# States in small groups, x cast by its load, transposes a batch ahead, outputs on another queue: a cross-attention and maxout kernel

## The chip, the cores and the metric

One core of a Trainium2 chip. The metric is the device time in microseconds of one execution, the median of several runs. A profile of one execution gives the times inside it; its span runs from the first to the last instruction.

## What is computed

For every batch b (8) and head h (8), with S = 512 tokens, Ns = 32 states and D = 64:

```
scores  = x @ state.T / 8          # 512 x 32
xread   = softmax(scores) @ state  # 512 x 64
scores2 = state @ x.T / 8          # 32 x 512
sread   = softmax(scores2) @ x     # 32 x 64
a = concat(xread, sread)           # 544 tokens, heads side by side: 512 features
out = max(a @ w1, a @ w2, a @ w3) @ w_out     # 512 -> 768 -> 512
```

All inputs and outputs are float32; x is 8.4 MB, the four weight matrices 6.3 MB together, the output 8.9 MB.

## The kernel before, in words

The kernel works in bf16 and batch by batch. Tokens stand four to a partition row (`J = 4`), heads in pairs: `g` is the position in a pair, `s` the pair. The states stand transposed in block-diagonal pairs (`bd`), so that one 128-row operand serves both scores and the products with the weights.

The steps of a batch, each a helper:

- `load_x(b)` (L75): x from HBM to bf16 by a casting DMA on GpSimd's queue.
- `x_transpose` (L153, on PE, with a copy from PSUM by the engine handed in) or `x_transpose_dma` (L165, a DMA transpose on SP's queue): xT.
- `scores` (L169): 16 matmuls of 64 columns (L181), then exp on ACT (L186) into `e`. `softmax` (L188): sum (L193) and reciprocal (L195) on DVE, multiplication into `a` on the engine handed in (L196; GpSimd from batch 2 on).
- `a_transpose` (PE, L201) or `a_transpose_dma` (SP, L210): aT.
- `g_cols(b, ms)` (L236): G, the states of the batch times columns of the weights. One m (128 of the 768 hidden columns) is 8 small matmuls (L244) and a copy from PSUM by ACT of 768 columns (L248).
- `x_maxout(b, m)` (L266): six matmuls of 512 columns (L258) into three PSUM tiles `pw`; ACT casts the first (L262), DVE takes two maxima (L263, L264) into `ht`.
- `sread(b)` (L215): 32 matmuls, two DVE operations, and a DMA transpose on SP into `ats`. At the end `s_maxout` puts the rows of all batches through the weights.
- `ffn_out(b, j)` (L276): six matmuls (L281), a copy to `osb` by ACT (L288), and for every two j an output DMA (L297) on SP.

The tiles `pw` and all transposes share four PSUM buffers; `pg`, `ps` and the keep-busy matmuls share two pairs of banks. The order of each engine's and each queue's work is the order of the program text (`manual_schedule`). The top part (L303 to L339) writes out batch 0 and the preparation of batch 1. From L343 on, `x_maxout(b, m)` for six m is followed by what stands in `slots[m]`: the preparation of batch n = b + 1, and `ffn_out` of the batch before from `pending`.

The states are prepared twice: `states_first` (L122) for batch 0, `states_rest` (L132) for all others, called after the first maxout of batch 0 (L316). `keep_busy(n)` (L113) issues n matmuls of 512 columns on zeros. Weights come in three chunks of hidden columns, (0,1), (1,3), (3,6), each three casting DMAs on GpSimd.

Of the kernel before, what the change touches and what calls it, by code (L numbers as in the profile page):

```python
# [8 lines left out]
F32 = mybir.dt.float32  # L9
# [6 lines left out]
def kernel(  # L16
# [36 lines left out]
    ctx.enter_context(tc.manual_schedule())  # L53


    st0_f = data.tile([128, 2, D], F32, name="st0f")
    nc.scalar.dma_start(out=st0_f, in_=state[0].rearrange("h n d -> (h n) d").rearrange("(t p) d -> p t d", p=128))
    x0_f = [data.tile([128, HS, J * D], F32, name=f"x0f{g}") for g in range(2)]
    for g in range(2):
        nc.sync.dma_start(  # L60
            out=x0_f[g], in_=x[0].rearrange("(s g) (p j) d -> g p s (j d)", g=2, j=J)[g])
    st_f = data.tile([128, 16, D], F32, name="stf")
    nc.sync.dma_start(
        out=st_f, in_=state.rearrange("b h n d -> (b h n) d").rearrange("(p t) d -> p t d", t=16))

    zero = const.tile([128, 512], BF16, name="zero")
    nc.vector.memset(zero, 0.0)
    ident = const.tile([128, 128], BF16, name="ident")
    make_identity(nc, ident)


    x_sb = [data.tile([128, XW + D], BF16, name=f"x{b}") for b in range(B)]
# [4 lines left out]
            out=x_sb[b][:, 0:XW].rearrange("p (h jd) -> p h jd", h=H),  # L77
            in_=x[b].rearrange("h (p j) d -> p h (j d)", j=J))

    chunks = ((0, 1), (1, 3), (3, 6))  # L80
    w_sb = [wpool.tile([128, HS, 3, (m1 - m0) * 128], BF16, name=f"w{m0}") for m0, m1 in chunks]
    wout_sb = wpool.tile([128, NM, d_model], BF16, name="wout")

# [13 lines left out]
    load_w(1)
    bd0 = data.tile([128, H, 2, Ns], BF16, name="bd0")
    nc.vector.memset(bd0, 0.0)
    bdr = data.tile([128, B - 1, H, 2, Ns], BF16, name="bdr")  # L100
    for b in range(B):
        nc.vector.memset(x_sb[b][:, XW:XW + D], 1.0)
    load_w(2)
    load_x(1)
    nc.gpsimd.dma_start(out=wout_sb, in_=moe_w_out.rearrange("(kk p) f -> p kk f", p=128))
    nc.gpsimd.memset(bdr, 0.0)
    load_x(2)

    warm = const.tile([128, 1], F32, name="warm")
    nc.scalar.activation(out=warm, in_=zero[:, 0:1], func=AF.Exp, scale=1.0)  # L110
# [6 lines left out]


    def bd(b, h):
        return bd0[:, h] if b == 0 else bdr[:, b - 1, h]  # L120

    def states_first():  # L122
        st0 = data.tile([128, 2, 2, D], BF16, name="st0")
        nc.vector.tensor_copy(out=st0, in_=st0_f.unsqueeze(2).to_broadcast((128, 2, 2, D)))
        p = pp.tile([128, 2, 128], BF16, tag="pw", bufs=4, name="pt0")
        for t in range(2):
            nc.tensor.transpose(p[:, t, :], st0[:, t].rearrange("p c d -> p (c d)"), ident)
        for c, copy in enumerate((nc.vector.tensor_copy, nc.scalar.copy)):
            r = slice(64 * c, 64 * c + 64)
            copy(out=bd0[r, :, c, :], in_=p[r].rearrange("p t (h n) -> p (t h) n", n=Ns))  # L130

    def states_rest():  # L132

        st = data.tile([128, 16, 2, D], BF16, name="st")
        nc.vector.tensor_copy(out=st[:, :, 0, :], in_=st_f)
        nc.scalar.copy(out=st[:, :, 1, :], in_=st_f)
        for k in range(2):
            p = pp.tile([128, 8, 128], BF16, tag="pw", bufs=4, name="pt")
            for t in range(8):
                nc.tensor.transpose(p[:, t, :], st[:, 8 * k + t].rearrange("p c d -> p (c d)"), ident)  # L140
            for c, copy in enumerate((nc.vector.tensor_copy, nc.scalar.copy)):
                r = slice(64 * c, 64 * c + 64)
                dst = bdr[r, :, :, c, :].rearrange("p b h (q t) -> p (b h) q t", t=16)
                copy(out=dst[:, :, :, 8 * k:8 * k + 8],
                     in_=p[r, :, 16:16 * B].rearrange("p t (k q) -> p k q t", q=2))
# [64 lines left out]
    def a_transpose_dma(b):  # L210
        new(aT, b, [128, J, 2, 128], "aT")
        nc.sync.dma_start_transpose(  # L212
            out=aT[b].rearrange("p j g t -> p (j g) t"), in_=a[b].rearrange("p j g s n -> p (j g s n)"))

    def sread(b):  # L215

        p = pp.tile([128, 2, 2, D], F32, tag="pw", bufs=4, name="psr")
        for j in range(J):
            for g in range(2):
                for s in range(HS):  # L220
                    xj = xv[b][:, 2 * s + g, j, :]
                    both = bass.AP(xj.tensor, xj.offset,
                                   (xj.ap[0], (XW - ((2 * s + g) * J + j) * D, 2), (1, D)))
                    nc.tensor.matmul(  # L224
                        p[32 * s:32 * s + 32, g], e[b][:, j, g, s, :], both,
                        start=(j == 0 and g == 0), stop=(j == J - 1), skip_group_check=True,
                        tile_position=(0, 32 * s))
        rd = work.tile([128, 2, 1], F32, tag="rd", name="rd")
        nc.vector.reciprocal(out=rd, in_=p[:, :, 1, 0:1])
        sr = work.tile([128, 2, D], BF16, tag="sr", name="sr")  # L230
        nc.vector.tensor_mul(out=sr, in0=p[:, :, 0, :], in1=rd.to_broadcast((128, 2, D)))
        nc.sync.dma_start_transpose(
            out=ats[:, b].rearrange("p s n -> p (s n)"), in_=sr.rearrange("p g d -> p (g d)"))


    def g_cols(b, ms):  # L236
        for m in ms:
            if m == 0:
                new(G, b, [128, 2, NM * 384], "G")
            w, f = w_cols(m)  # L240
            p = pp.tile([128, 2, 512], F32, tag="two", name="pg")
            for s in range(HS):
                for g in range(2):
                    nc.tensor.matmul(  # L244
                        p[32 * s:32 * s + 32, g, 0:384].rearrange("p (i f) -> p i f", i=3),
                        bd(b, 2 * s + g)[64 * g:64 * g + 64, g, :], w[64 * g:64 * g + 64, s, :, f],
                        start=True, stop=True, tile_position=(64 * g, 32 * s))
            nc.scalar.copy(out=G[b][:, :, m * 384:(m + 1) * 384], in_=p[:, :, 0:384])  # L248


    def maxout(b, m, n, lhs, rhs, nk):
# [24 lines left out]
    def ffn_out(b, j, split=False):  # L276
# [47 lines left out]
    g_cols(0, (5,))
    x_maxout(0, 5)
    x_transpose(1, 0, act)
    x_transpose(1, 1, dve)
    x_transpose_dma(2)
    scores(1, 0, 2)
    softmax(1, 0, 2, nc.vector.tensor_mul)  # L330
    load_x(3)
    sread(1)
    g_cols(1, (0, 1))
    ffn_out(0, 0)
    g_cols(1, (2, 3))
    ffn_out(0, 1)
# [68 lines left out]
```

## Time and profile before

| | us |
|---|---|
| median of 3 runs | 180.58 |
| lowest, highest run | 179.66, 521.62 |
| the profiled execution | 182.44 |
| its span | 180.7 |

The profiled execution is one run; the rows of its trace are set against its own time. The rows below come from its page and from views of its trace: a table of stretches, the chain of work that ended last, the waits, the groups of instructions by form, and the landings of DMAs. A group's mean duration of matmuls is longer than their distance, since they are pipelined.

### The profile page before, as it was taken

Reading aid. Unit: us, or ns where it says so; the run is one execution under the profiler, and the core shown is the slowest. Engines: PE = TensorE matmul, PEld = TensorE weight load, DVE = VectorE, ACT = ScalarE, POOL = GpSimd, SP = SyncE. Lnnn points to the kernel's source line nnn. Section 1 sums busy time; section 2 is a strip of 40 time slices with the busy share of each in tenths; the row PEclk is TensorE's granted clock in tenths of the full one; section 3 lists DMA queues with packets and bytes.
Section 4 is the critical chain, followed back from the end, with each engine's and each line's share of the span. In section 5 each row is a group of like instructions: output and inputs, shape, how many; then the busy total and the mean of one; then the engine's idle time right before and its main releaser. Section 6 shows DMA issues by size and latency. Waiting matters only on the chain.

```text
span 180.7 us, 3477 instructions
## 1 busy us (share of the span) xinstructions
PE 154.4 (85%) x1388; PEld 71.5 (40%) x1403; DVE 96.1 (53%) x167; ACT 98.7 (55%) x155; POOL 31.8 (18%) x34
## 2 busy tenths in 40 slices
PE   5646788679997599979997999799999999999991
PEld 1421532334442334323433343334334447566440
DVE  2475535762856365537653765376547638555200
ACT  3353446559928174758275937483865583344240
POOL 8895000000240033002300320040004000000040
PEclk9999999999999889999999999999999999999999
DMA  5999999802049805980599069903660332020354
GB/s 149 290 196 202 204 195 194 104 4 110 19 42 225 148 4 61 211 233 29 52 212 269 0 64 201 268 2 120 111 190 0 123 62 118 0 116 0 119 193 158
DMA packets 37168, 22.57 MB, mean 125 GB/s; under 512 B 22624, under 2 KB 34656, under 8 KB 37152
## 3 DMA queue, kind: packets, MB, share of 16 engines
q1 hardware_dynamic: 23936, 15.21, 33.4%
q0 software_dynamic: 12944, 7.08, 29.9%
q8 instruction: 11, 0.18, 0.4%
q10 hardware_dynamic: 272, 0.07, 0.2%
q14 instruction: 5, 0.04, 0.1%
HBM read 15.27 MB, written 8.91 MB: 134 GB/s over the span
## 4 chain that ended last, share of the span: by engine, by line
PE 50%; DMA 18%; DVE 14%; ACT 9%; SPq 4%; issue 3%; DVEq 0%; ACTq 0%
PE pw L258 28%; PE po L281 14%; DMA xT<-x 11%; DVE t L263 4%; DVE den L193 3%; ACT e L186 3%; DVE ht L264 3%; DMA x0f<-in_x_dram 3%; SPq L212 3%; DMA aT<-a 3%; PE ps L181 2%; PE psr L224 2%; ACT t L262 2%; ACT G L248 2%; PE pg L244 1%
## 5 line engine op out<-in xcount | busy, mean ns | idle before, releaser
L258 PE MATMUL pw<-aT,G 128*128 128x512 bf16 x288 | 75.7, 398 | 10.7 <-DMA aT<-a 6.2
L263 DVE TENSOR_TENSOR t<-t,pw 128x512 bf16<-128x512 bf16 (+1 forms) x54 | 35.1, 650 | 50.5 <-ACT t L262 43.9
L281 PE MATMUL po<-wout,ht 128*128 128x512 bf16 x189 | 48.0, 380 | 0.8
L258 PEld LDWEIGHTS <-G 128*128 128x128 bf16 x288 | 27.6, 101 | 47.5 <-issue 9.0
L262 ACT CAST t<-pw 128x512 bf16<-128x512 f32 (+1 forms) x54 | 30.6, 566 | 25.3 <-PE pw L258 23.9
L248 ACT CAST G<-pg 128x768 bf16<-128x768 f32 x48 | 36.2, 806 | 10.2 <-PE pg L244 9.8
L264 DVE TENSOR_TENSOR ht<-t,pw 128x512 bf16<-128x512 bf16 (+1 forms) x54 | 35.5, 658 | 5.6
L288 ACT COPY osb<-po 128x512 f32<-128x512 f32 x33 | 19.3, 586 | 22.3 <-PE po L281 21.8
L196 POOL TENSOR_TENSOR a<-e,rden 128x1024 bf16<-128x1024 bf16 x6 | 11.4, 1904 | 107.6 <-DVE rden L195 62.5
L281 PEld LDWEIGHTS <-ht 128*128 128x128 bf16 x204 | 18.4, 97 | 24.5 <-issue 5.5
L193 DVE TENSOR_REDUCE den<-e 128x32 f32<-128x1024 bf16 (+1 forms) x9 | 9.9, 1100 | 6.4 <-ACT e L186 6.4
L186 ACT ACTIVATE e<-ps 128x1024 bf16<-128x1024 f32 x7 | 7.2, 1023 | 7.7 <-PE ps L181 7.6
L244 PE MATMUL pg<-w,bdr 64*32 64x384 bf16 x336 | 10.9, 328 | 0.0
L258 PE MATMUL pw<-ats,w 128*128 128x256 bf16 x72 | 8.8, 273 | 0.0
L292 POOL DMA_DIRECT2D out_dram<-osb x4 | 2.1, 523 | 35.3 <-ACT osb L288 35.1
L258 PEld LDWEIGHTS <-w 128*128 128x128 bf16 x72 | 7.0, 98 | 2.1
L87 POOL DMA_DIRECT2D w<-in_moe_w_dram x9 | 7.5, 856 | 0.6 <-DMA w<-in_moe_w_dram 0.5
L181 PEld LDWEIGHTS <-xT 128*128 128x128 bf16 x128 | 5.3, 106 | 5.5 <-DMA xT<-x 3.7
L181 PE MATMUL ps<-bdr,xT 128*128 128x64 bf16 x112 | 5.1, 201 | 1.9 <-DMA xT<-x 1.1
L76 POOL DMA_DIRECT2D x<-in_x_dram x7 | 6.4, 928 | 0.0
L224 PE MATMUL psr<-x,e 128*32 128x128 bf16 x256 | 5.5, 232 | 1.1 <-ACT e L186 1.1
L244 PEld LDWEIGHTS <-bdr 64*32 64x32 bf16 x336 | 3.1, 89 | 8.3 <-issue 8.0
(47 smaller groups left out, 55.8 us busy)
## 6 DMA issues: line engine op xcount, KB each, us to landing
out_dram<-osb SPq DMA_DIRECT2D x15, 512.0 KB, 2.9
x<-in_x_dram POOLq DMA_DIRECT2D x7, 512.0 KB, 6.6
w<-in_moe_w_dram POOLq DMA_DIRECT2D x3, 384.0 KB, 10.4
x0f<-in_x_dram SPq DMA_DIRECT2D x2, 512.0 KB, 4.8
w<-in_moe_w_dram POOLq DMA_DIRECT2D x3, 256.0 KB, 8.0
wout<-in_moe_w_out_dram POOLq DMA_DIRECT2D x1, 768.0 KB, 17.0
stf<-in_state_dram SPq DMA_DIRECT2D x1, 512.0 KB, 6.2
out_dram<-osb SPq DMA_DIRECT2D x2, 256.0 KB, 2.3
```

What stands on the lines that cost most here:

```text
L181: nc.tensor.matmul(p[:, 2 * jj:2 * jj + 2, g - g0, s, :], xT[b][:, h, jj, :], bd(b, h).rearrange("p c n -> p (c n)"), start=(g == g0 and s ...
L186: nc.scalar.activation(out=e[b][:, :, g0:g1], in_=p, func=AF.Exp, scale=scale)
L193: nc.vector.reduce_sum(out=den, in_=e[b][:, :, g0:g1], axis=AX.X)
L196: mul(out=a[b][:, :, g0:g1].rearrange("p j g s n -> p j (g s) n"), in0=e[b][:, :, g0:g1].rearrange("p j g s n -> p j (g s) n"), in1=rden.r ...
L244: nc.tensor.matmul(p[32 * s:32 * s + 32, g, 0:384].rearrange("p (i f) -> p i f", i=3), bd(b, 2 * s + g)[64 * g:64 * g + 64, g, :], w[64 * ...
L248: nc.scalar.copy(out=G[b][:, :, m * 384:(m + 1) * 384], in_=p[:, :, 0:384])
L258: nc.tensor.matmul(p[:, 0:n], lhs(i, k), rhs(k), start=(k == 0), stop=(k == nk - 1))
L262: nc.scalar.copy(out=t0[:, 0:n], in_=pw[0][:, 0:n])
L263: nc.vector.tensor_max(t1[:, 0:n], t0[:, 0:n], pw[1][:, 0:n])
L264: nc.vector.tensor_max(ht[b][:, m, :], t1[:, 0:n], pw[2][:, 0:n])
L281: nc.tensor.matmul(p, ht[b][:, m, j * 128:(j + 1) * 128], wout_sb[:, m, :], start=(m == 0), stop=(m == NM - 1))
L288: nc.scalar.copy(out=o[:, j, :], in_=p)
```

## The change

- The states come in four groups of two batches. Group 0 is loaded first, on SP; groups 1 to 3 on ACT's queue after the first G columns of batch 0. Group 1 is transposed at the end of batch 0's part, groups 2 and 3 in batches 2 and 4 (slot 3), with ACT for the casts and copies. `states_rest` and its place go.
- x of batch 0 is loaded by two casting DMAs, the first on GpSimd's queue, ahead of the identity and the weights; the casts on DVE and ACT go.
- Weight chunks are (0,1), (1,3), (3,4), (4,6); the last two, x of batch 2 and w_out are issued after the first softmax, whose multiplication GpSimd does.
- Keep-busy blocks are 6, 3 and 6 matmuls in place of 5.
- Batch 2 is transposed on PE too. From batch 3 on the DMA transpose of x is issued a batch earlier (slot 0, and slot 3 of batch 1 for batch 3), that of a in slot 2 in place of 3, and those of the sread results are collected and issued in slot 4.
- `g_cols` takes the engines of its copies; in batch 0's part DVE does some of them. Preparation of batch 1 is mixed with the maxouts of batch 0, and its `ffn_out` calls all move to batch 1.
- Outputs of batches 0 to 6 go on GpSimd's queue.

```diff
+    def load_st(k, eng):
+        eng.dma_start(
+            out=st_f[k],
+            in_=state[2 * k:2 * k + 2].rearrange("b h n d -> (b h n) d").rearrange("(p t) d -> p t d", t=4))
+    st_f = [data.tile([128, 4, D], F32, name=f"stf{k}") for k in range(B // 2)]
+    load_st(0, nc.sync)
...
+    for g in range(2):
+        nc.gpsimd.dma_start(
+            out=x_sb[0][:, 0:XW].rearrange("p (s g jd) -> g p s jd", g=2, s=HS)[g],
+            in_=x[0].rearrange("(s g) (p j) d -> g p s (j d)", g=2, j=J)[g])
...
-    chunks = ((0, 1), (1, 3), (3, 6))
+    chunks = ((0, 1), (1, 3), (3, 4), (4, 6))
...
+    def states(k, cast, copy):
+        st = work.tile([128, 4, 2, D], BF16, tag="st", name="st")
+        cast(out=st, in_=st_f[k].unsqueeze(2).to_broadcast((128, 4, 2, D)))
+        p = pp.tile([128, 4, 128], BF16, tag="pw", bufs=4, name="pt")
+        for t in range(4):
+            nc.tensor.transpose(p[:, t, :], st[:, t].rearrange("p c d -> p (c d)"), ident)
+        for c in range(2):
             r = slice(64 * c, 64 * c + 64)
+            copy(out=bds[k][r, :, :, c, :].rearrange("p b h (q t) -> p (b h) q t", t=4),
+                 in_=p[r].rearrange("p t (k q) -> p k q t", q=8))
...
+        late.append(lambda: nc.sync.dma_start_transpose(
+            out=ats[:, b].rearrange("p s n -> p (s n)"), in_=sr.rearrange("p g d -> p (g d)")))
...
-            nc.sync.dma_start(
+            (nc.sync if b == B - 1 else nc.gpsimd).dma_start(
...
-    keep_busy(5)
-    states_first()
-    dve(out=xv[0].rearrange("p (s g) j d -> p g s (j d)", g=2)[:, 0], in_=x0_f[0])
-    act(out=xv[0].rearrange("p (s g) j d -> p g s (j d)", g=2)[:, 1], in_=x0_f[1])
+    keep_busy(6)
+    states(0, dve, act)
+    keep_busy(3)
     x_transpose(0, 0, dve)
     x_transpose(0, 1, dve)
-    for g in range(2):
-        scores(0, g, g + 1)
-        softmax(0, g, g + 1, nc.vector.tensor_mul)
+    scores(0, 0, 1)
+    softmax(0, 0, 1, nc.gpsimd.tensor_mul)
+    load_w(2)
+    load_w(3)
+    load_x(2)
+    nc.gpsimd.dma_start(out=wout_sb, in_=moe_w_out.rearrange("(kk p) f -> p kk f", p=128))
+    scores(0, 1, 2)
+    softmax(0, 1, 2, nc.vector.tensor_mul)
     g_cols(0, (0,))
+    for k in range(1, B // 2):
+        load_st(k, nc.scalar)
+    keep_busy(6)
     a_transpose(0, 0, act)
     a_transpose(0, 1, dve)
     x_maxout(0, 0)
-    states_rest()
+    g_cols(0, (1, 2), (act, dve))
     sread(0)
-    g_cols(0, (1, 2))
     x_maxout(0, 1)
+    x_transpose(1, 0, dve)
+    x_transpose(1, 1, act)
     x_maxout(0, 2)
-    g_cols(0, (3, 4))
+    scores(1, 0, 2)
+    softmax(1, 0, 2, nc.gpsimd.tensor_mul)
+    load_x(3)
+    g_cols(0, (3,))
+    g_cols(1, (0,), (dve,))
     x_maxout(0, 3)
+    g_cols(0, (4, 5))
+    sread(1)
     x_maxout(0, 4)
...
+    g_cols(1, (1, 2), (act, dve))
     a_transpose(1, 0, act)
     a_transpose(1, 1, dve)
+    x_maxout(0, 5)
+    g_cols(1, (3, 4), (act, dve))
+    states(1, act, act)
...
-    pending = [(0, 2), (0, 3)]
+    pending = [(0, j) for j in range(J)]
     for b in range(1, B):
         n = b + 1
         slots = [[] for _ in range(NM)]
         if n < B:
-            slots[0].append(lambda: scores(n, 0, 2))
-            slots[0].append(lambda: softmax(n, 0, 2, nc.gpsimd.tensor_mul))
-            slots[1].append(lambda: g_cols(n, (0, 1)))
+            if n == 2:
+                slots[0].append(lambda: x_transpose(2, 0, act))
+                slots[0].append(lambda: x_transpose(2, 1, dve))
+                slots[1].append(lambda: g_cols(1, (5,)))
+                slots[3].append(lambda: x_transpose_dma(3))
+            if 2 < n < B - 1:
+                slots[0].append(lambda: x_transpose_dma(n + 1))
+            at = 1 if n == 2 else 0
+            slots[at].append(lambda: scores(n, 0, 2))
+            slots[at].append(lambda: softmax(n, 0, 2, nc.gpsimd.tensor_mul))
+            slots[2 if n == 2 else 1].append(lambda: g_cols(n, (0, 1)))
+            slots[2].append(lambda: a_transpose_dma(n))
             slots[3].append(lambda: sread(n))
-            slots[3].append(lambda: a_transpose_dma(n))
             slots[4].append(lambda: g_cols(n, (2, 3)))
             slots[5].append(lambda: g_cols(n, (4, 5)))
-            if n + 1 < B:
-                slots[4].append(lambda: x_transpose_dma(n + 1))
+            slots[4].append(late_transposes)
+            if n % 2 and n + 1 < B:
+                slots[3].append(lambda: states((n + 1) // 2, act, act))
             if n + 2 < B:
-                slots[1].append(lambda: load_x(n + 2))
+                slots[0].append(lambda: load_x(n + 2))
```

## Rows read from the trace of the kernel before

**Rows 1.** The page: TensorE's busy time, share of the span and matmuls.

```profile
PE 154.4 (85%) x1388; PEld 71.5 (40%) x1403; DVE 96.1 (53%) x167; ACT 98.7 (55%) x155; POOL 31.8 (18%) x34
```

**Rows 2.** Stretches cut at first pw matmuls: bounds, length, busy times, clock, DMA share, GB/s.

```profile
0.00:13.56 13.56, 7.27 (x55) 4.12 (x56) 6.87 (x21) 5.37 (x8) 12.32 (x18) 1.00 1.12 212
13.56:43.69 30.13, 23.24 (x257) 10.86 (x257) 15.84 (x25) 16.60 (x24) 2.40 (x3) 1.00 0.94 136
43.69:60.67 16.98, 13.47 (x144) 5.77 (x144) 9.96 (x16) 10.98 (x17) 2.80 (x2) 1.00 0.64 125
60.67:79.25 18.58, 17.48 (x154) 7.46 (x157) 10.05 (x16) 10.98 (x17) 2.79 (x2) 0.91 0.66 100
79.25:114.64 35.39, 32.34 (x309) 13.41 (x313) 20.11 (x32) 21.96 (x34) 5.59 (x4) 1.00 0.76 136
114.64:147.91 33.27, 32.00 (x308) 13.57 (x313) 20.10 (x32) 21.10 (x33) 3.81 (x2) 1.00 0.39 108
147.91:180.70 32.79, 28.59 (x166) 16.32 (x167) 13.20 (x25) 11.75 (x24) 2.07 (x4) 1.00 0.27 97
```

**Rows 3.** The chain that ended last, in the front: start, us, what.

```profile
0.74 0.45 SPq L60
...
12.41 0.70 DVE a L196
...
19.18 2.09 DVE bdr L144 x2
...
23.08 4.44 PE pw L258 x10
...
29.14 2.76 PE pw L258 x12
```

**Rows 4.** The same chain in batches 4 to 6.

```profile
111.00 5.30 DMA xT<-x
...
133.07 0.65 PE ps L181 x16
...
134.86 1.23 DVE den L193
...
138.52 1.29 PE po L281 x6
139.81 1.29 PE pw L258 x6
141.11 0.56 PE psr L224 x32
...
143.08 0.45 PE pg L244 x16
```

**Rows 5.** Waits: engine, line, releaser, total us, times, longest us.

```profile
PE pw L258 <- DMA aT<-a: 6.2, 4, 3.3
```

**Rows 6.** Groups by form: shapes, count, busy us, mean ns, idle before.

```profile
L248 ACT CAST G<-pg 128x768 bf16<-128x768 f32 x48 | 36.2, 806 | 10.2 <-PE pg L244 9.8
L264 DVE TENSOR_TENSOR ht<-t,pw 128x512 bf16<-128x512 bf16 x48 | 33.0, 687 | 5.0
...
L262 ACT CAST t<-pw 128x512 bf16<-128x512 f32 x48 | 28.3, 590 | 21.3 <-PE pw L258 21.3
...
L196 POOL TENSOR_TENSOR a<-e,rden 128x1024 bf16<-128x1024 bf16 x6 | 11.4, 1904 | 107.6 <-DVE rden L195 62.5 <-ACT G L248 45.1
...
L264 DVE TENSOR_TENSOR ht<-t,pw 128x256 bf16<-128x256 bf16 x6 | 2.5, 422 | 0.6
...
L163 DVE COPY xT<-pxt 128x1024 bf16<-128x1024 bf16 x3 | 2.1, 689 | 1.6 <-PE pxt L160 1.6
```

**Rows 7.** SP's first transpose of x, a load's issue, landings of aT.

```profile
30.06 3.09 SPq L167 DMA_TRANSPOSE xT<-x  x1
...
104.11 0.94 POOL L76 DMA_DIRECT2D x<-in_x_dram  x1
...
DMA to landing us min/median/max: 3.1/4.7/4.9
```

More of the change, by code (lines that the diff above doesn't have):

```diff
@@ L53 @@
     ctx.enter_context(tc.manual_schedule())
-    st0_f = data.tile([128, 2, D], F32, name="st0f")
-    nc.scalar.dma_start(out=st0_f, in_=state[0].rearrange("h n d -> (h n) d").rearrange("(t p) d -> p t d", p=128))
-    x0_f = [data.tile([128, HS, J * D], F32, name=f"x0f{g}") for g in range(2)]
-    for g in range(2):
-        nc.sync.dma_start(
[L61 to L69, printed above, removed]
+    def load_st(k, eng):
[4 more added lines that the diff above has]
+    load_st(0, nc.sync)
     x_sb = [data.tile([128, XW + D], BF16, name=f"x{b}") for b in range(B)]
@@ L78, in load_x @@
             in_=x[b].rearrange("h (p j) d -> p h (j d)", j=J))
-    chunks = ((0, 1), (1, 3), (3, 6))
+    for g in range(2):
+        nc.gpsimd.dma_start(
+            out=x_sb[0][:, 0:XW].rearrange("p (s g jd) -> g p s jd", g=2, s=HS)[g],
+            in_=x[0].rearrange("(s g) (p j) d -> g p s (j d)", g=2, j=J)[g])
+    ident = const.tile([128, 128], BF16, name="ident")
+    make_identity(nc, ident)
+    zero = const.tile([128, 512], BF16, name="zero")
+    nc.vector.memset(zero, 0.0)
+    chunks = ((0, 1), (1, 3), (3, 4), (4, 6))
     w_sb = [wpool.tile([128, HS, 3, (m1 - m0) * 128], BF16, name=f"w{m0}") for m0, m1 in chunks]
@@ L96 @@
     load_w(0)
[L97 to L100, printed above, removed]
+    bds = [data.tile([128, 2, H, 2, Ns], BF16, name=f"bd{k}") for k in range(B // 2)]
+    for k in range(B // 2):
+        nc.vector.memset(bds[k], 0.0)
     for b in range(B):
         nc.vector.memset(x_sb[b][:, XW:XW + D], 1.0)
-    load_w(2)
+    load_w(1)
     load_x(1)
-    nc.gpsimd.dma_start(out=wout_sb, in_=moe_w_out.rearrange("(kk p) f -> p kk f", p=128))
-    nc.gpsimd.memset(bdr, 0.0)
-    load_x(2)
     warm = const.tile([128, 1], F32, name="warm")
@@ L119, in bd @@
     def bd(b, h):
[L120 to L128, printed above, removed]
-            r = slice(64 * c, 64 * c + 64)
[L130 to L145, printed above, removed]
+        return bds[b // 2][:, b % 2, h]
+    def states(k, cast, copy):
[5 more added lines that the diff above has]
+        for c in range(2):
+            r = slice(64 * c, 64 * c + 64)
+            copy(out=bds[k][r, :, :, c, :].rearrange("p b h (q t) -> p (b h) q t", t=4),
+                 in_=p[r].rearrange("p t (k q) -> p k q t", q=8))
     xT, e, a, aT, G, ht, osb = {}, {}, {}, {}, {}, {}, {}
@@ L213, in a_transpose_dma @@
             out=aT[b].rearrange("p j g t -> p (j g) t"), in_=a[b].rearrange("p j g s n -> p (j g s n)"))
+    late = []
     def sread(b):
@@ L229, in sread, with g_cols @@
         nc.vector.reciprocal(out=rd, in_=p[:, :, 1, 0:1])
-        sr = work.tile([128, 2, D], BF16, tag="sr", name="sr")
+        sr = work.tile([128, 2, D], BF16, tag="sr", bufs=B, name="sr")
         nc.vector.tensor_mul(out=sr, in0=p[:, :, 0, :], in1=rd.to_broadcast((128, 2, D)))
[L232 to L237, printed above, removed]
+        late.append(lambda: nc.sync.dma_start_transpose(
+            out=ats[:, b].rearrange("p s n -> p (s n)"), in_=sr.rearrange("p g d -> p (g d)")))
+    def g_cols(b, ms, copies=(nc.scalar.copy, nc.scalar.copy)):
+        for m, copy in zip(ms, copies):
             if m == 0:
@@ L247, in g_cols @@
                         start=True, stop=True, tile_position=(64 * g, 32 * s))
-            nc.scalar.copy(out=G[b][:, :, m * 384:(m + 1) * 384], in_=p[:, :, 0:384])
+            copy(out=G[b][:, :, m * 384:(m + 1) * 384], in_=p[:, :, 0:384])
     def maxout(b, m, n, lhs, rhs, nk):
@@ L296, in ffn_out, with late_transposes @@
         if j == 1 or j == 3 or j0 == j:
-            nc.sync.dma_start(
+            (nc.sync if b == B - 1 else nc.gpsimd).dma_start(
                 out=out[b * SP:b * SP + S, :].rearrange("(p j) f -> p j f", j=J)[:, j0:j + 1, :],
                 in_=o[:, j0:j + 1, :])
+    def late_transposes():
+        while late:
+            late.pop(0)()
     dve, act = nc.vector.tensor_copy, nc.scalar.copy
-    keep_busy(5)
-    states_first()
-    dve(out=xv[0].rearrange("p (s g) j d -> p g s (j d)", g=2)[:, 0], in_=x0_f[0])
-    act(out=xv[0].rearrange("p (s g) j d -> p g s (j d)", g=2)[:, 1], in_=x0_f[1])
+    keep_busy(6)
+    states(0, dve, act)
+    keep_busy(3)
     x_transpose(0, 0, dve)
     x_transpose(0, 1, dve)
-    for g in range(2):
-        scores(0, g, g + 1)
-        softmax(0, g, g + 1, nc.vector.tensor_mul)
+    scores(0, 0, 1)
[6 more added lines that the diff above has]
+    softmax(0, 1, 2, nc.vector.tensor_mul)
     g_cols(0, (0,))
+    for k in range(1, B // 2):
+        load_st(k, nc.scalar)
+    keep_busy(6)
     a_transpose(0, 0, act)
@@ L315 @@
     x_maxout(0, 0)
-    states_rest()
+    g_cols(0, (1, 2), (act, dve))
     sread(0)
-    g_cols(0, (1, 2))
     x_maxout(0, 1)
+    x_transpose(1, 0, dve)
+    x_transpose(1, 1, act)
     x_maxout(0, 2)
-    g_cols(0, (3, 4))
+    scores(1, 0, 2)
[3 more added lines that the diff above has]
+    g_cols(1, (0,), (dve,))
     x_maxout(0, 3)
+    g_cols(0, (4, 5))
+    sread(1)
     x_maxout(0, 4)
[L324 to L336, printed above, removed]
+    g_cols(1, (1, 2), (act, dve))
     a_transpose(1, 0, act)
     a_transpose(1, 1, dve)
-    g_cols(1, (4, 5))
-    pending = [(0, 2), (0, 3)]
+    x_maxout(0, 5)
+    g_cols(1, (3, 4), (act, dve))
+    states(1, act, act)
+    pending = [(0, j) for j in range(J)]
     for b in range(1, B):
```

## The prediction

> **What bounds the kernel now.** I read the page first, then the table of stretches cut at the first pw matmul of each batch, then the chain that ended last, then the waits, the groups by form and the DMA landings. TensorE is busy 154.4 of 180.7 us [rows 1], so it is the engine to fill, but the 26 us of gaps are not spread evenly [rows 2]. The stretch from the first pw matmul of batch 0 to that of batch 1 takes 30.13 us with PE busy for 23.2 of them, and much of that busy time is slow. The chain shows why [rows 3]: after the first maxout comes the preparation of all other states (two DVE copies alone from 19.18 for 2.09, between casts, transposes and ACT copies), and the second maxout starts only at 23.08. There 10 pw matmuls take 4.44 us, 0.44 each; at 29.14, 12 take 2.76, 0.23 each. For 512 columns these are the two levels of TensorE's clock, 1.2 and 2.4 GHz. The granted-clock column reads 1.00 in both places, so in this front I go by the spacing. It rose after 4.4 us of matmuls back to back.
>
> From batch 2 on the chain has another pattern [rows 4]: each batch passes through a DMA transpose of x (5.30 us from issue to landing) before its scores start. The first matmuls of four batches also waited for the transpose of a, 6.2 us in all [rows 5]. Batches 3 and 4 take 17.7 us each, batches 5 and 6 16.6, and batch 2 takes 18.58 at a granted clock of 0.91, the lower level having come back after a wait of 3.3 us at its border [rows 2, 5]. The last stretch, 32.79 us, is dense matmul work and the last outputs.
>
> **The front, to the first pw matmul** (13.56 us now). x of batch 0 goes straight to bf16 by its DMA, so a DVE and an ACT cast go, and PE gets a keep-busy block of 3 ahead of the transposes, which takes back most of this: at 0.44 each, 1.3 us. No row has x of batch 0 on a casting queue: its transposes could start earlier by the casts (about 1.0) or later by two GpSimd issues (0.94 each [rows 7]); with the keep-busy block as a floor under them I take no change for the scores. Then the softmax of group 0 is multiplied on GpSimd, which frees DVE of one of its two multiplications: the second, at 12.41 for 0.70 now [rows 3], moves up by as much. But 6 keep-busy matmuls (2.6 us slow, 1.4 fast) now stand ahead of the transposes of a on PE, and three state loads are issued in ACT's stream (0.45 us each by the nearest DMA issue [rows 3]). Together the first pw matmul falls between 13.1 and 15.0; I take 14.0, **+0.4**.
>
> **Batch 0 to batch 1** (30.13 us now). Removed: the whole states_rest block, and two ffn_out calls, which batch 1 takes. Added: half of the transposes, scores and softmax of batch 1 move between its maxouts, and one group of states. I count each engine's work between the two marks. PE at the fast level: 6 maxouts at 1.29, ten G columns at 0.225 (half of a pair's 0.45), two sreads at 0.56, scores 0.65 [rows 4], with about 2.2 for 28 transposes (an estimate: 128 columns at the fast spacing are 0.06, I take 0.08), makes 14.0. ACT: 6 t casts at 0.59, 6 G copies at 0.81 [rows 6], the exp and a copy of xT at about 1.0 each, aT 0.6, and the states (a cast and two copies of 512 columns, 0.6 each like the t casts) makes 12.8. DVE: 12 maxima at 0.69 = 8.2; 4 G copies, a form that the trace does not have on DVE. Nearest are the maxima with a PSUM operand, 0.42 for 256 columns and 0.69 for 512 [rows 6]; continued to 768 this gives 0.95 (ends: 0.52, the rate of the bf16 copy of xT from PSUM, 0.69 for 1024, and 1.27, three times the short maximum), so 3.8. With the reduction 1.2 [rows 4], reciprocal 0.35, the second xT copy 0.7, aT 0.4 and two sreads' ends 0.9, DVE has 15.6. **DVE is the longest** where PE was. Walking the order by hand, with DVE starting 1.0 after the first matmul and the states' ACT work at the end, I get 17.1. PE's clock: the new keep-busy blocks leave it few gaps from about 5 us on, and I expect the fast level before or during the first maxout; I add 0.8 for half a maxout at the slow one. 17.9, **-12.2**.
>
> The loads must keep up. Up to the landing of x of batch 2 at 30.0, when SP's transpose of it starts [rows 7], 9.9 MB were read (the page's sizes are those written; the bf16 ones are read as f32), some 355 GB/s from about 2 us on. In the new order on GpSimd (x0, w of m 0, w of 1 and 2, x1, then w 3, w 4 and 5, x2, wout) the same rate lands w 1-2 at 12.5, x1 at 15.5, w 3 at 18, w 4-5 at 23, wout at 30. They are wanted at 15.3, 17.6, 21, 24 and 35. The fourth has one microsecond to spare.
>
> **Batch 1** (16.98 us now, 3.3 of it the wait for aT). It gets two more ffn_out (2.6 at 1.29 each [rows 4]), the x transposes of batch 2 on PE (1.1), a fifth G column (0.2), and loses the wait. 6 maxouts 7.74, 4 ffn_out 5.16, seven G columns 1.6, scores 0.65, sread 0.56, transposes 1.1 make 16.8, **-0.2**.
>
> **Batches 2 to 6** (18.58 + 35.39 + 33.27 = 87.24 us now [rows 2]). PE's own work is 6 x 1.29 + 4 x 1.29 + 3 x 0.45 + 0.65 + 0.56 = 15.5 [rows 4]. In batch 6 the first maxout began at 131.19, so scores could start at 132.5 and started at 133.07: 0.55 of the 16.6 is the wait for xT. What remains, 16.1, has 0.6 in which the reduction on DVE holds up the maxima behind it; the change leaves that in. xT is now issued in slot 0 a batch ahead, some 16 us before it is wanted, and lands after 5.3. The transpose of a moves from slot 3 to slot 2, ahead of the sread transposes: the reduction starts 3.7 us into the batch, so the GpSimd multiplication (1.9 [rows 6]) ends about 7.4 into it, and 4.9, the longest landing in the trace [rows 7], puts aT at 12.5 of 16.1. Two of these batches carry a group of states: 4 transposes on PE, 0.5, ACT's 1.8 in its slack (busy 21.1 of 33.3 [rows 2]). The drop of the clock in batch 2 goes with the wait ahead of it. 5 x 16.1 + 1.0 = 81.5, **-5.7**.
>
> Outputs on GpSimd: a load's issue there takes 0.94 [rows 7], and two outputs make 1.9 us a batch on an engine busy 5.6 of 35.4 [rows 2]. The last of a batch waits for ACT's copy to the batch's border, and the next multiplication starts 5.5 us after it. Nothing, with that cover. The last stretch: nothing.
>
> The Trainium skill ("Trainium Kernel Development and Optimization", Key Constraints) says that DMAs from the SP, ACT and POOL queues run on the same 16 engines, so that several issuers save only issue time. The trace does not decide how much: aT landed in 3.1 to 4.9 us [rows 7]. By the rule the outputs' move gives the transposes no bandwidth; the sum above asks for none, and the third rival is what it would do if the engines were full.
>
> **Sum.** 0.4 - 12.2 - 0.2 - 5.7 = -17.7 us. The profiled execution took 182.44 (span 180.7 and 1.74 around it): 164.7. The median of the runs, 180.58, is 1% below the profiled time, and 17.7 off that gives 162.9. Between the two: **164 us**. Its own range is 160 to 168 (the DVE copies' ends are -1.7 and +1.3, the first matmul's -0.9 and +1.0, the two bases 1.8).
>
> **Rivals.**
> 1. *The slow clock lasts through batch 0.* For it: the front's matmuls came 0.44 apart until 27.5 although PE was busy 23 of 30 us, and the new front still has waits on softmax. Against: three keep-busy blocks and no state stall. Then the six maxouts cost 15.7 instead of 7.7, and the smaller work about half more: PE needs 23 to 24 in place of 17.9, so 170. Chance 0.14.
> 2. *The loads end last in batch 0.* GpSimd issues 0.94 apiece, x0 ahead of everything, and w 4-5 has one microsecond. A start of the stream 2 us later and a rate 10% lower put it at 27.5, 3.5 late: 167.5. Chance 0.12.
> 3. *The transposes slow down among loads and outputs* and the waits of batches 2 to 6 stay: the load of x and an output now run beside aT. For it: aT took 3.1 alone and 4.7 to 4.9 in company. If it doubled to 9.4, it would land at 16.8 plus its queue, about a microsecond late in each batch, and all of the 5.7 would be lost: 170. Chance 0.07.
> 4. *Slower than before: GpSimd's stream holds up the softmax.* An output stands on GpSimd until ACT has copied; what is behind it (loads, the next multiplication) stands too, then aT, then the next batch's pw. Slack to aT is 16.1 - 12.5 = 3.6 us. It decides when the multiplication starts more than that late; for 184 us each of six batches must lose (17.7 + 2) / 6 = 3.3, so 6.9 us of blocking a batch, where 1.9 of issuing and 0.6 of ACT's copy are seen. 186 us. Chance 0.03.
>
> **Chances.** Forecast 0.64, rivals 0.14, 0.12, 0.07, 0.03. The first four are all faster by over 2%, which is about what a measurement of this kernel can tell from no change: faster 0.94; the mixture of 3 and 4 with 1 could end near no change, 0.03; slower 0.03. The range takes in rivals 1 to 3: 159 to 171.
>
> **What would show it.** Right: first pw matmul near 14; the first of batch 1 near 32, with DVE busiest between them; pw spacing 0.22 from the second maxout on; batches 2 to 6 near 16.1 with no wait of scores on a DMA and SP idle behind the x transpose; last stretch 32.8. Wrong: matmuls 0.43 apart beyond 17 us (rival 1); G columns or transposes idle for w or x (2); pw of a batch released by aT (3); GpSimd's multiplication waiting behind an output (4); or DVE copies of G far from 0.95.

## The result, and the profile after

The changed kernel takes 165.87 us (median of 4 runs, 165.27 to 166.65) against 181.13 for the kernel before in the same comparison: a ratio of 0.918, 95% interval 0.910 to 0.927. The ratio leaves out one execution of the kernel before that took 521.62 us, where its others took 179.66 to 181.69. The forecast was 164, its range 159 to 171. The profiled execution took 166.65 us with a span of 164.8, so it is 15.8 shorter than the profiled one before; 17.7 were forecast.

The page of the changed kernel: TensorE is busy 4.8 us less than in [rows 1] and fills a larger share of the span.

```profile
PE 149.6 (91%) x1427; PEld 69.9 (42%) x1427; DVE 96.6 (59%) x168; ACT 98.9 (60%) x158; POOL 42.5 (26%) x54
```

The table of stretches of the changed kernel, cut at first pw matmuls as in [rows 2] (columns: bounds, length, busy time of PE, PEld, DVE, ACT, POOL with counts, granted clock, DMA share, GB/s):

```profile
0.00:12.04 12.04, 8.04 (x68) 4.18 (x68) 7.80 (x22) 5.23 (x8) 10.20 (x18) 1.00 1.14 142
12.04:32.28 20.24, 14.59 (x225) 6.97 (x224) 14.41 (x25) 10.95 (x16) 8.40 (x10) 1.00 1.43 204
32.28:50.22 17.94, 17.65 (x183) 7.87 (x181) 10.97 (x18) 13.20 (x20) 2.53 (x2) 1.00 0.55 105
50.22:67.19 16.97, 16.48 (x162) 6.93 (x161) 10.05 (x16) 12.57 (x21) 3.91 (x4) 1.00 0.73 146
67.19:99.88 32.69, 32.23 (x318) 13.87 (x317) 20.10 (x32) 23.44 (x38) 7.80 (x8) 1.00 0.78 147
99.88:132.13 32.25, 31.85 (x313) 13.73 (x312) 20.11 (x32) 21.76 (x35) 6.08 (x6) 1.00 0.39 102
132.13:164.84 32.71, 28.75 (x169) 16.35 (x167) 13.20 (x25) 11.77 (x24) 3.60 (x7) 1.00 0.27 97
```

Against [rows 2]: the front is 1.5 us shorter, batch 0 9.9, batch 1 1.0 longer, batches 2 to 6 together 81.9 instead of 87.24, the last stretch the same. These add up to -15.8. In batch 0 PE is busy for 14.59 us, close to the 14.0 counted ahead, but the stretch is 20.24 long. What it waits for stands in PE's timeline of the front (start, us, engine, line, operation, out<-in, form, count, and in brackets the idle time before and what ended it):

```profile
6.89 0.62 PE L145 MATMUL pxt<-ident,x 128*128 128x128 bf16 x8 [0.53 <-DMA x<-in_x_dram]
7.34 0.40 PE L166 MATMUL psh<-bd,xT 128*128 128x64 bf16 x8
...
9.38 0.36 PE L231 MATMUL pg<-w,bd 64*32 64x384 bf16 x8 [0.68 <-DMA w<-in_moe_w_dram]
9.67 1.47 PE L114 MATMUL idle<-zero 128*128 128x512 bf16 x6
...
12.04 1.46 PE L245 MATMUL pw<-aT,G 128*128 128x512 bf16 x6 [0.45 <-ACT aT L193]
13.98 0.52 PE L231 MATMUL pg<-w,bd 64*32 64x384 bf16 x16 [0.49 <-DMA w<-in_moe_w_dram]
...
17.85 1.07 PE L145 MATMUL pxt<-ident,x 128*128 128x128 bf16 x16 [1.12 <-DMA x<-in_x_dram]
...
21.20 0.36 PE L231 MATMUL pg<-w,bd 64*32 64x384 bf16 x8 [0.52 <-DMA w<-in_moe_w_dram]
...
25.23 0.52 PE L231 MATMUL pg<-w,bd 64*32 64x384 bf16 x16 [1.27 <-DMA w<-in_moe_w_dram]
```

The first pw matmuls come 0.22 us apart at once (6 in 1.46): the six keep-busy matmuls before them ran at the fast level already. But PE waits for every load that batch 0 still needs, 0.5 to 1.3 us each time: three times for weights and once for x of batch 1. The chain that ended last goes through the last of them, and later through one transpose of x, the first by DMA:

```profile
10.58 3.69 POOL w L89 x5
14.27 10.82 DMA w<-in_moe_w_dram
25.09 0.14 issue
25.23 0.40 PE pg L231 x8
...
44.04 7.82 DMA xT<-x
51.86 0.05 issue
51.91 0.65 PE ps L166 x16
```

After that no batch waits for xT or aT, and the transposes have gone from the chain of [rows 4] and from the waits of [rows 5]. The groups by form price two things that the rows of the kernel before did not show, an output's issue on GpSimd (553 ns) and a copy of G by DVE (938 ns):

```profile
L284 POOL DMA_DIRECT2D out_dram<-osb x14 | 7.7, 553 | 75.2 <-ACT osb L275 73.3 <-ACT t L249 1.8
...
L235 DVE CAST G<-pg 128x768 bf16<-128x768 f32 x4 | 3.8, 938 | 0.0
```

### The profile page after: what moved, and what is told of

The parts are those of the page before. It is cut to its first block, busy times and chain, and to the rows that moved or that the text cites. A ratio compares the mean times of both kernels' runs of the same rounds, so it can differ in the third digit from the quotient of the medians.

```text
span 164.8 us, 3552 instructions
## 1 busy us (share of the span) xinstructions
PE 149.6 (91%) x1427; PEld 69.9 (42%) x1427; DVE 96.6 (59%) x168; ACT 98.9 (60%) x158; POOL 42.5 (26%) x54
## 4 chain that ended last, share of the span: by engine, by line
PE 56%; DMA 15%; DVE 11%; ACT 7%; issue 4%; POOL 4%; DVEq 0%; ACTq 0%; POOLq 0%
PE pw L245 28%; PE po L268 20%; DMA w<-in_moe_w_dram 7%; DMA xT<-x 5%; DVE den L178 4%; PE pg L231 4%; ACT e L171 4%; DVE ht L251 3%; DVE t L250 3%; DMA x<-in_x_dram 3%; POOL w L89 2%; PE ps L166 2%; PE psr L211 1%; DMA out_dram<-osb 1%; ACT t L249 1%
## 5 line engine op out<-in xcount | busy, mean ns | idle before, releaser
L245 PE MATMUL pw<-aT,G 128*128 128x512 bf16 x288 | 71.5, 379 | 2.6 <-DVE ht L251 1.2
L245 PEld LDWEIGHTS <-G 128*128 128x128 bf16 x288 | 26.8, 98 | 34.6 <-issue 4.5
L235 ACT CAST G<-pg 128x768 bf16<-128x768 f32 x44 | 33.3, 801 | 12.3 <-PE pg L231 11.9
L275 ACT COPY osb<-po 128x512 f32<-128x512 f32 x33 | 19.3, 586 | 20.8 <-PE po L268 20.2
L284 POOL DMA_DIRECT2D out_dram<-osb x14 | 7.7, 553 | 75.2 <-ACT osb L275 73.3
L181 POOL TENSOR_TENSOR a<-e,rden 128x1024 bf16<-128x1024 bf16 (+1 forms) x8 | 14.4, 1799 | 35.6 <-DVE rden L180 22.5
L231 PE MATMUL pg<-w,bd 64*32 64x384 bf16 x384 | 12.8, 328 | 3.2 <-DMA w<-in_moe_w_dram 3.0
L231 PEld LDWEIGHTS <-bd 64*32 64x32 bf16 x384 | 3.6, 88 | 13.5 <-issue 13.5
L89 POOL DMA_DIRECT2D w<-in_moe_w_dram x12 | 9.0, 773 | 0.0
L129 ACT COPY bd<-pt 64x512 bf16<-64x512 bf16 x8 | 4.6, 580 | 4.7 <-PE pt L126 4.6
L114 PE MATMUL idle<-zero 128*128 128x512 bf16 x15 | 5.2, 492 | 1.2 <-DVE zero L80 1.2
```

The costliest lines, as they stand in the source:

```text
L89: nc.gpsimd.dma_start(out=w_sb[c][:, :, i, :], in_=w.rearrange("(kk p) f -> p kk f", p=128)[:, :, m0 * 128:m1 * 128])
L181: mul(out=a[b][:, :, g0:g1].rearrange("p j g s n -> p j (g s) n"), in0=e[b][:, :, g0:g1].rearrange("p j g s n -> p j (g s) n"), in1=rden.r ...
L231: nc.tensor.matmul(p[32 * s:32 * s + 32, g, 0:384].rearrange("p (i f) -> p i f", i=3), bd(b, 2 * s + g)[64 * g:64 * g + 64, g, :], w[64 * ...
L245: nc.tensor.matmul(p[:, 0:n], lhs(i, k), rhs(k), start=(k == 0), stop=(k == nk - 1))
L275: nc.scalar.copy(out=o[:, j, :], in_=p)
```

## The experiments

All runs, by the stretches of their profiled execution (us). The ratio is to executions of the kernel before that were taken beside the run, with its 95% interval.

| kernel | median us | ratio | first pw | batch 0 | batch 1 | batches 2-6 | span |
|---|---|---|---|---|---|---|---|
| before | 181.13 | 1 | 13.56 | 30.13 | 16.98 | 87.24 | 180.7 |
| the change | 165.87 | 0.918 (0.910-0.927) | 12.04 | 20.24 | 17.94 | 81.91 | 164.8 |
| outputs on SP | 165.94 | 0.913 (0.907-0.920) | 12.10 | 19.76 | 17.95 | 81.91 | 164.6 |
| late issue | 172.1 | 0.947 (0.941-0.954) | 11.88 | 19.51 | 17.93 | 87.34 | 169.4 |
| both | 176.32 | 0.970 (0.964-0.977) | 12.18 | 19.22 | 21.84 | 87.20 | 173.3 |
| no keep-busy | 165.6 | 0.912 (0.906-0.918) | 12.31 | 19.20 | 17.93 | 81.51 | 163.6 |
| one weight chunk | 163.95 | 0.905 (0.900-0.910) | 14.64 | 17.44 | 17.95 | 81.81 | 164.5 |
| x0 on SP | 165.17 | 0.913 (0.907-0.918) | 12.69 | 18.34 | 17.61 | 81.98 | 163.4 |
| states in a block | 172.32 | 0.950 (0.944-0.956) | 14.36 | 24.34 | 18.26 | 81.20 | 170.8 |
| no mixing | 176.14 | 0.972 (0.966-0.979) | 12.36 | 27.96 | 19.15 | 82.03 | 174.2 |
| softmax later | 164.14 | 0.906 (0.902-0.910) | 12.39 | 19.21 | 17.94 | 79.66 | 161.9 |
| front edits | 164.32 | 0.906 (0.902-0.910) | 13.78 | 16.57 | 17.70 | 81.51 | 162.8 |
| all of these | 162.14 | 0.894 (0.891-0.898) | 12.69 | 17.52 | 17.71 | 79.66 | 160.2 |
| all, no keep-busy | 163.46 | 0.900 (0.896-0.904) | 13.48 | 18.01 | 17.71 | 79.65 | 161.7 |

The same code took 19.2 to 20.2 us for batch 0 in different runs (the four rows behind the kernel before, and the softmax later, differ only behind batch 0), so a microsecond there is no verdict. In these five runs batch 1 begins at 31.39 to 32.28.

**Outputs back on SP.**

```diff
-            (nc.sync if b == B - 1 else nc.gpsimd).dma_start(
+            nc.sync.dma_start(
```

> The changed kernel with all outputs back on SP's queue; nothing else. Theory A (the transposes gained because they are issued earlier, not because outputs left the queue): on SP the x transpose of slot 0 and the transpose of a in slot 2 still stand ahead of the outputs of their slots, so batches 2 to 6 stay at 82.1 us within 0.7 and the span at 164.8 within 1. Rival B (the outputs in SP's queue, which wait for ACT's copies, were what made the transposes late): batches 2 to 6 go up by 2 to 5 us and scores or pw wait for xT or aT in most of them.

Batches 2 to 6 take 81.91 us with either queue. The move to GpSimd by itself is worth nothing, as theory A has it. The landings of aT were 5.7 us in the middle with outputs on GpSimd and 5.6 on SP, where the kernel before had 4.7 (its range is in [rows 7]). The slow ones go with a load of x: in the change, the three transposes of a that were issued within 0.1 us of such a load (at 57.46, 74.01 and 90.14) landed after 7.4, 7.9 and 7.4 us, the other three, with an output beside them, after 4.0, 3.6 and 3.1. With the outputs on SP it is the same, 7.5 to 8.0 and 3.1 to 3.8; the queue that an output is issued on does not show. That agrees with the rule of the Trainium skill that the prediction weighed ("Trainium Kernel Development and Optimization", Key Constraints).

**Late issue**, outputs on GpSimd.

```diff
-            if 2 < n < B - 1:
-                slots[0].append(lambda: x_transpose_dma(n + 1))
...
-            slots[2].append(lambda: a_transpose_dma(n))
             slots[3].append(lambda: sread(n))
+            slots[3].append(late_transposes)
+            slots[3].append(lambda: a_transpose_dma(n))
...
-            slots[4].append(late_transposes)
+            if 2 < n < B - 1:
+                slots[4].append(lambda: x_transpose_dma(n + 1))
```

> The changed kernel with the issue points of the kernel before: transposes of x in slot 4, of a in slot 3 behind that of the sread result; outputs stay on GpSimd. Theory A (issue point): xT is wanted about 17.4 us after the start of a batch and lands at 18 to 19, aT lands at the border; batches 2 to 6 return to 86 to 87.5 us (+4 to +5.4), span 169 to 170. Rival B (queue of the outputs): most of the gain stays, batches 2 to 6 at 82 to 84, span below 167.

Batches 2 to 6 take 87.34 us: the whole 5.4 is lost, as theory A has it. PE waits for both transposes again, as in the kernel before (engine, line, releaser: us, times, longest):

```profile
PE pw L245 <- DMA aT<-a: 2.9, 3, 1.4
...
PE ps L166 <- DMA xT<-x: 1.7, 4, 0.7
```

The edit moves the transposes of x, of a and of the sread results together; no run takes them apart.

**Both edits.** The diffs are the two above.

> Both of the two edits before: late issue points and outputs on SP. By A the same as late issue alone, 86 to 87.5 us in batches 2 to 6, within 0.7 of it. By B the whole loss, +5, comes only here. A drop of the granted clock after a long wait, as in batch 2 of the kernel before, would add 1 to 1.5.

Batches 2 to 6 come out the same, 87.20. But batch 1 takes 3.9 us more, which neither theory had placed there. SP's rows show how. With outputs on GpSimd (the late issue alone) nothing stands on SP ahead of the transpose of x of batch 3, and it ran early, at 33.59:

```profile
33.59 3.19 SPq L152 DMA_TRANSPOSE xT<-x  x1
36.83 8.55 SPq L219 DMA_TRANSPOSE ats<-sr  x3
45.49 1.25 SPq L197 DMA_TRANSPOSE aT<-a  x1
```

With outputs on SP the first output of batch 0 stands ahead, waits for ACT's copy, and the whole line follows it; aT is issued 4.6 us later, and the first pw matmul of batch 2 waits 3.75 us for it:

```profile
41.88 0.34 SPq L284 DMA_DIRECT2D out_dram<-osb  x1
42.34 3.33 SPq L152 DMA_TRANSPOSE xT<-x  x1
45.73 4.23 SPq L219 DMA_TRANSPOSE ats<-sr  x3
50.07 1.26 SPq L197 DMA_TRANSPOSE aT<-a  x1
```

So the queue of the outputs counts where a transpose stands behind an output whose copy comes late, as rival B has it, and in this kernel that is this one place: in batches 2 to 6 outputs stand ahead of transposes on SP too, and the time is the same.

**No second and third keep-busy block.** Both calls are left out.

> The changed kernel without its second and third keep-busy block (3 and 6 matmuls). Theory A (they bring the fast level to batch 0): the first pw matmuls come 0.43 us apart for one to three maxouts, batch 0 gets 1.3 to 4 us longer, the first pw matmul starts 0 to 0.7 earlier; span 166 to 168.5. Rival (batch 0 is bounded by the weights' landing at 25.1 us, so slow matmuls before it are hidden): pw slow, but the first pw of batch 1 within 0.5 of 32.3, span 164.5 to 165.3.

The first six pw matmuls come 0.42 us apart, the granted clock reads 0.84 in the front and 0.92 in batch 0, and yet the first pw matmul of batch 1 starts at 31.51, before the 32.28 of the change, and the median is the same (165.6 for 165.87). The rival has the mechanism: while loads end last, the slow level is hidden. The span of 163.6 us lies below even its 164.5 to 165.3; theory A's 166 to 168.5 did not come.

**One weight chunk.**

```diff
-        return w_sb[c], slice(f, f + 128)
+        return w_sb[0], slice(0, 128)
...
-    load_w(1)
...
-    load_w(2)
-    load_w(3)
```

> Leaves out work: only the weights of the first 128 hidden columns are loaded, and all six column groups use them, so the output is not the reference's; 3.9 MB of reads go, the instructions of PE, ACT and DVE stay. Theory A (batch 0 at 20.2 us instead of the 17.9 forecast because weights and x landed late): batch 0 comes to 17.0 to 18.0 us, the first pw matmul stays at 12.0 or falls to 11.5, span 162 to 163. Rival (hand-offs between DVE, ACT and PE set batch 0): it stays above 19.3.

Batch 0 comes to 17.44 us, inside A's bounds; the hand count had 17.1 and 0.8 for the clock.

```profile
14.64:32.08 17.44, 14.77 (x224) 6.95 (x224) 14.43 (x25) 10.95 (x16) 3.68 (x3) 1.00 0.77 117
```

PE waits for no load in this stretch any more. But the 2.8 us to the change are not the price of the loads, for the front of this profiled execution was late (it is the longest of four, 166.33, the others 163.7 to 164.0): PE had to wait for the first weights until 10.71, the keep-busy block then ran at the slow level, 6 matmuls in 2.55, and the first pw matmul came at 14.64, not at A's 11.5 to 12.0.

```profile
10.71 0.36 PE L228 MATMUL pg<-w,bd 64*32 64x384 bf16 x8 [2.01 <-DMA w<-in_moe_w_dram]
11.00 2.55 PE L111 MATMUL idle<-zero 128*128 128x512 bf16 x6
```

So batch 1 begins at 32.08, hardly earlier than in the change; loads had 2.6 us more to land before batch 0 began. The other three executions give the price better: their spans are 161.9 to 162.2, those of the change 163.5 to 164.8, so the missing loads are worth about 2 us.

**x of batch 0 on SP**, in float32, with the two casts of the kernel before.

```diff
-        nc.gpsimd.dma_start(
-            out=x_sb[0][:, 0:XW].rearrange("p (s g jd) -> g p s jd", g=2, s=HS)[g],
-            in_=x[0].rearrange("(s g) (p j) d -> g p s (j d)", g=2, j=J)[g])
+        nc.sync.dma_start(
+            out=x0_f[g], in_=x[0].rearrange("(s g) (p j) d -> g p s (j d)", g=2, j=J)[g])
...
+    dve(out=xv[0].rearrange("p (s g) j d -> p g s (j d)", g=2)[:, 0], in_=x0_f[0])
+    act(out=xv[0].rearrange("p (s g) j d -> p g s (j d)", g=2)[:, 1], in_=x0_f[1])
```

> The changed kernel with x of batch 0 loaded in float32 on SP and cast by DVE and ACT, as before; weights then come first on GpSimd's queue. If the casting load helps the front: first pw matmul 1 to 2 us later than 12.0, batch 0 the same, span 165.5 to 167. If the load stream is what counts (its first bytes start earlier from two queues): first pw about 12.5 to 13, but w and x of batch 1 land 0.5 to 1.5 earlier, batch 0 19 to 19.5, span 164 to 165.

The second pattern, and more of it: the first pw matmul is 0.65 later, batch 0 takes 18.34 with a single wait for w of 0.7 us left, and batch 1 begins at 31.03, earlier than in any run with the code of the change there. The last weights land at 23.84 in place of 25.09: with x on SP they no longer stand behind it on GpSimd's queue. Over the whole kernel the gain is not clear of noise (ratios 0.913 and 0.918, with intervals that overlap); what can be said is that the casting load brings no gain.

**States in a block** after the first maxout.

```diff
     x_maxout(0, 0)
+    states(1, dve, act)
+    states(2, act, dve)
+    states(3, dve, act)
...
-    states(1, act, act)
...
-            if n % 2 and n + 1 < B:
-                slots[3].append(lambda: states((n + 1) // 2, act, act))
```

> The changed kernel with the groups 1 to 3 of the states in one block after the first maxout of batch 0, casts and copies on DVE and ACT. Theory A (the block stands on the path, as in the kernel before, where 17.3 to 22.2 us went to it): batch 0 gets 2 to 4 us longer, batches 1, 2 and 4 together 1 to 2 shorter; span 165.5 to 167.5. Rival (the loads end last in batch 0 and hide it): batch 0 grows by less than 1, span 163 to 165.

Batch 0 grows by 4.1 us, just over A's 2 to 4, to

```profile
14.36:38.70 24.34, 17.26 (x233) 8.17 (x232) 15.07 (x27) 12.60 (x20) 6.48 (x7) 0.86 0.98 139
```

and the granted clock falls to 0.86 in it: while the casts and copies pass between the engines PE stands three times, for 1.7 to 1.95 us, and the six pw matmuls of the second maxout then take 2.48, at the slow level. Theory A has the direction and the place, but it made the block too cheap: the four executions have spans of 169.3 to 170.9, all above its 165.5 to 167.5. In the profiled one 2.3 of the 6.0 us lie ahead of batch 0, where the keep-busy block was slow too, and batches 1 to 6 are only 0.4 shorter where A had 1 to 2.

**No mixing.** The preparation of batch 1 stands behind the maxouts of batch 0; the diff only moves the calls.

> The changed kernel with the preparation of batch 1 after the maxouts of batch 0 in place of between them. Theory A (mixing is the larger part of the gain of batch 0, since the preparation is a chain of x transposes, exp, reduction, multiplication, copies): batch 0 gets 5 to 8 us longer, span 169 to 172. Rival (the loads hide most): batch 0 grows by 2 to 4, span 167 to 169.

Batch 0 takes 7.7 more, within A's bounds, and batch 1 1.2 more at a clock of 0.89; the span of 174.2 is over A's 169 to 172. A had left out the clock: it reads 0.83 in batch 0, where the same matmuls now keep PE busy for 17.70 us in place of 14.59. Of the parts that were taken back one at a time this one costs the most.

**Softmax a slot later.**

```diff
-            slots[at].append(lambda: softmax(n, 0, 2, nc.gpsimd.tensor_mul))
+            slots[1].append(lambda: softmax(n, 0, 2, nc.gpsimd.tensor_mul))
```

> The changed kernel with the softmax of batch n called in slot 1 in place of slot 0 (its scores stay in slot 0). Theory A (of a batch's 16.13 us, 0.6 is DVE's reduction standing ahead of the maxima of the second maxout): batches 2 to 6 fall from 81.9 to 79.3 to 79.9, span 162 to 162.8. Rival (aT then becomes the bound: the multiplication ends about 9.6 us into the batch and aT landed in 5.7, up to 7.9, of a batch of 15.6): pw at the border waits for aT in the batches with a load of x, batches 2 to 6 at 80.5 to 83.

```profile
49.54:129.20 79.66, 79.54 (x789) 34.70 (x788) 49.79 (x80) 57.75 (x92) 17.76 (x18) 1.00 0.64 133
```

Batches 2 to 6 take 79.66 us, within theory A's bounds, and PE is busy for 79.54 of them. A plain batch falls from 16.13 to 15.76, and no border waits for aT.

**Front edits**: x of batch 0 on SP as above, and

```diff
+    states(1, nc.gpsimd.tensor_copy, act)
     x_maxout(0, 5)
     g_cols(1, (3, 4), (act, dve))
-    states(1, act, act)
...
-                slots[3].append(lambda: x_transpose_dma(3))
+                slots[1].append(lambda: x_transpose_dma(3))
```

> Three edits of the front: x of batch 0 by SP and casts; group 1 of the states cast by GpSimd and transposed ahead of the last maxout of batch 0; the DMA transpose of x of batch 3 in slot 1 of batch 1 in place of slot 3. If the load stream from two queues, ACT's casting of the states (1.3 us of waiting at 32.05) and the late xT (0.4) are what they seem: first pw 12 to 13, batch 0 17 to 17.8, batch 1 17.0 to 17.5, batch 2 16.5; span 161.5 to 162.8. Rival (the loads take back what hand-offs give): 163 to 164.

Batch 2 loses its wait (16.56), batch 0 is 16.57 but the first pw starts at 13.78, with a slow keep-busy block again (2.74). Batch 1 loses only 0.24, less than expected, and x of batch 0 on SP alone had already given 0.33 there.

**All of these** (the front edits and the softmax a slot later), and the same without the two keep-busy blocks.

> The three edits of the front and the softmax in slot 1 together. By A the gains add: span 159 to 160.5, batches 2 to 6 at 79.3 to 79.9. By the rival of the single run they do not: 161.5 or more.

```profile
0.00:12.69 12.69, 8.15 (x68) 3.77 (x69) 7.87 (x23) 6.16 (x9) 8.54 (x16) 1.00 1.16 195
12.69:30.21 17.52, 14.94 (x224) 6.93 (x224) 13.03 (x23) 10.80 (x17) 9.30 (x11) 1.00 1.43 205
30.21:47.92 17.71, 17.30 (x189) 7.85 (x181) 12.58 (x20) 12.73 (x19) 2.53 (x2) 1.00 0.72 131
47.92:127.58 79.66, 79.54 (x790) 34.67 (x789) 49.82 (x80) 57.77 (x92) 17.70 (x18) 1.00 0.64 131
```

The gains add: 162.14 us, faster than both kernels, with an interval (0.891 to 0.898) that does not meet that of the change.

> The same without the keep-busy blocks of 3 and 6. If batch 0 is still set by the landing of weights: first pw 12 to 12.5 with matmuls 0.42 apart, batch 0 within 0.5 of the run with the blocks, span within 0.7 of it. If the loads no longer hide the slow clock: batch 0 1 to 1.5 us longer.

The first pw matmul comes at 13.48, 0.8 later and outside the expected 12 to 12.5; batch 0 takes 0.5 more, as the first case had it, but the span is 1.4 longer where that case had at most 0.7. PE waits for no load in this batch 0, and the medians differ by 1.3 us: with the loads no longer last, the blocks are worth about a microsecond.

## Why the prediction was right, and where its steps were off

The mechanisms held, except for the time that the loads take, and the total came within 2 us: -15.8 in the profiled execution for -17.7. Part of that closeness is luck, since the front came out better than forecast and the stretches behind it worse.

*The front* (+0.4 forecast, -1.5 measured). The forecast left the scores where they were. They began at 7.34, where the kernel before has

```profile
8.50 0.63 PE L181 MATMUL psh<-bd,xT 128*128 128x64 bf16 x8
```

With x of batch 0 on SP and cast again they begin at 8.33, so the 1.0 us of the casts, which the forecast had set against two issues, was won. The fast level was there by 9.7 us, so the block of six cost 1.47 and not 2.6. The step was sized for a clock between the two levels. Three other runs, with the slow level in this block, put the first pw matmul at 13.8 to 14.6, which is within the range that the step gave.

*Batch 0* (-12.2 forecast, -9.9 measured). The count of work was right: PE 14.6 for 14.0, a DVE copy of G 0.94 for the 0.95 continued from the maxima, and 17.5 us in the run with all of the edits, where the loads come earlier, for the 17.9 forecast. DVE was not the longest, though, as the forecast had it: it is busy 14.41 us for the 15.6 counted, PE 14.59. The term that failed is "the fourth has one microsecond to spare". The stream was taken to start at 2 us with 355 GB/s. x of batch 0 was all there at 6.84, where that start gives 5.3, so everything behind it came 1.5 us late or more: the weights 4-5 at 25.1 instead of 23. An average rate fitted to one late landing hides a slow start. The rate was lower as well: x of batch 1, the weights and the other states, 6.2 MB read from then to 25.1, make some 340 GB/s (an estimate from these sizes). The second rival, with chance 0.12, had this mechanism, its sign (G columns and transposes idle for w and x) was seen, and a good half of its price came. The front's surplus and this loss belong together: batch 0 began 2.0 us earlier than forecast, the loads did not, and batch 1 began at 32.28, close to the 31.9 of the forecast. What the front had won beyond the forecast was given back as waiting.

*Batch 1* (-0.2 forecast, +1.0 measured). I summed PE's work alone. The first 4.5 us, with two maxouts and the transposes of x of batch 2, hold 3.7 of it. By the order of the work their copies from PSUM and the maxima hold back the four shared buffers, but the trace puts only 0.17 us of PE's waiting there down to a maximum, and no run tests it. The front edits took 0.24 off batch 1, x on SP alone 0.33, so the states' work on ACT is not shown to be a part of it. The cause of this microsecond stays open.

*Batches 2 to 6* (-5.7 forecast, -5.3 measured). Right in size and cause: late issue alone loses 5.4. A plain batch takes 16.13 where 16.1 was forecast, and of the 0.6 put down to the reduction on DVE, moving it gives 0.37 back. What was off is the landing beside a load of x, up to 7.9 for aT where 4.9 was the longest before; the slack covered it, except once, where xT of batch 3 took 7.8 and cost 0.4.

*Outputs on GpSimd* (nothing forecast, nothing measured). The cover named, the long idle time of GpSimd, held; what the move is worth appears only together with a late issue (176.32 against 172.1 us).

*The rivals.* The first (slow clock through batch 0) did not occur, and the run without the blocks shows that for the first maxouts it would have been hidden by the loads. Of the third the slower landing came, 7.4 to 7.9 us where the rival reckoned with 9.4, but not the loss: no pw at a border waited for aT. The fourth did not occur: the multiplication on GpSimd waited for DVE or ACT, not for an output's issue.

## What to carry to other kernels

An in-order queue is a line: place a transfer ahead of whatever in the line waits for another engine, and it runs as early as its data allow; which queue the rest uses then hardly matters. When a stall is filled with other work, look for what ends last next: here it was the landing of weights in a stretch that had been too slow to feel them. A long reduction does better behind a maxout that has much matmul work after it: here some 1.8 us of it in place of 0.5 gave 0.37 us a batch.

## What was not expected of the hardware

The same six keep-busy matmuls took 1.47 us in most runs and 2.55 to 2.74 in three of the eleven that have the block, all ending with the first pw matmul at 13.8 to 14.6, where the others have 11.9 to 12.7. In two of the three PE had waited 1.6 to 2.0 us for weights just before, in the third it had not. That third one, the front edits, and x of batch 0 on SP run the same code up to there, and their matmuls start within 0.03 us of each other from the first score on, yet the block took (x on SP first)

```profile
9.90 1.47 PE L114 MATMUL idle<-zero 128*128 128x512 bf16 x6
...
9.93 2.74 PE L114 MATMUL idle<-zero 128*128 128x512 bf16 x6
```

What else decides it stays open.
